# Fused adaLN, attention and gated MLP on one core: how the first modulation weights and V's weights are read and used

## The chip, the core and the metric

The kernel runs on one core of a Trainium2 chip. A core has a matrix engine (TensorE, "PE" in the profile; its weight loads are shown as "PEld"), a vector engine (VectorE, "DVE"), a scalar engine (ScalarE, "ACT"), a general engine (GpSimd, "POOL") and a sync engine (SyncE, "SP") that issues most transfers. Each engine works through its own list of instructions in order; an instruction that waits holds up all that stand behind it on that engine. Matrix products land in PSUM, which has eight banks; everything else lives in SBUF or in device memory. The metric is the device time of one execution in microseconds (us).

## The reference

With one sequence of 2048 rows, width 448 and 16 heads of 28:

```python
mod = silu(c) @ w_mod            # c: 1x448, w_mod: 448 x 6*448, six parts sa, ca, ga, sb, cb, gb
h = layernorm(x) * (1 + ca) + sa
x = x + ga * attention(h)        # attention(h): qkv = h @ wqkv, softmax over 2048 keys, @ wo
h = layernorm(x) * (1 + cb) + sb
x = x + gb * gated_mlp(h)
```

Everything is float32. The change concerns the first pair of parts, sa and ca, and the product of the first 512 rows of h with the columns of wqkv that make V.

## The kernel before

The kernel's order of work is written out by hand: the instructions of each engine run in the order in which the program issues them. The rows of x are taken in four groups of 512 (four tiles of 128 rows). The start, up to the first product for q and k, does this for group 0:

- `load_x(0)` (L178) brings the four tiles of x: tiles 0 and 1 by one transfer each from ACT's queue, tiles 2 and 3 together from SP's. `load_mod(0)` (L173) brings the part of w_mod for (sa, ca) as four blocks `wm` of 112x896, one for each 112 of the 448 entries of c; each block has all 448 columns of sa and of ca. Four transfers of V's weights (`load_w("v", i)`, chunks of 128 rows of wqkv in the order 0, 2, 1, 3, the last one 64 rows in two transfers) follow on SP, and then group 1 of x and the first columns of the weights of q and k (`load_w("a", i)`).
- `ln_stat`, `ln_rs`, `ln_norm` (L274 to L298) make the layer norm: means and variances on DVE, the power -1/2 on POOL, the normalization on DVE, and a copy of 64 columns on ACT. `tp_first` (L369) transposes tile by tile on PE into the four banks `tps[0..3]`, one for each chunk of 128 columns.
- The modulation columns: the product silu(c) @ w_mod is a sum over the four blocks. The first block is scaled on ACT (L380), blocks 1 and 2 are added on DVE for all 896 columns (`mod_acc`, L241), block 3 chunk by chunk (`mod_last`, L407). `mod_dot` (L420) sums over the 112 partitions on PE by a product with ones, and `mod_cols` (L427, L429) brings the result from PSUM into `col_ca` and `col_sa` on DVE. A chunk's columns can therefore be ready only after all four blocks have come.
- h itself is kept as a rounded high part and a low remainder (fp32r), in `hT[0]`, whose slots 0, 1, 2, 6 hold the high parts of chunks 0 to 3 and slots 3, 4, 5 the remainders of chunks 0 to 2 (slot 6 holds both for the short chunk 3). `h_hi` (L441) makes the high part on ACT, `h_full` (L436) the full value on DVE, `h_lo` (the helper `sub`, L84) the remainder. V's weights are split in the same way into `wv`: `wv_hi` (L354 on ACT, L352 on POOL for chunk 2) and `wv_lo` (`sub`, L84, on DVE).
- `v_step` (L477) runs the products for V: eleven pairs of slots, four row tiles each, 44 matrix products of 128x448. The order `order` goes through high parts first: pairs (0,0), (2,2), (1,1) and then the pairs with remainders.
- Between these, `pe_fill` (L230) lets PE multiply x by ones with no use made of the result: 14 such products at the start, and 5, 2, 2 and 4 later. Each is two passes of PE.

Then `qk_unit` (L323) begins the products for q and k, and the attention and the MLP follow.

Of the kernel before, what the change touches and what calls it, by code (L numbers as in the profile page):

```python
# [8 lines left out]
F32 = mybir.dt.float32  # L9
# [24 lines left out]
def tile_adaln_mha_gmlp(ctx, tc, x, wqkv, wo, w_in, w_spT, b_sp, w_out, cT, w_mod, out):  # L34
# [22 lines left out]
    cols = {}  # L57
# [5 lines left out]
    heapF = dpool.tile([128, 4 * 896], F32R, name="heapF", tag="heapF")  # L63
# [16 lines left out]

    wqk = Halves(4, hview(heapD[2], 0, 4, 896), hview(heapF, 0, 4, 896))
# [85 lines left out]
    def bank(name):  # L167
        k = mode[0](name) if mode[0] else banks[0]
        banks.remove(k)
        banks.append(k)  # L170
        return ring.tile([128, 512], F32, name=name, tag=f"b{k}")

    def load_mod(pair, eng):  # L173
        for k in range(4):
            wms[pair, k] = e1.tile([112, 2, D], F32, name="wm", tag=("wm", "wm", "raw")[pair], bufs=4)
            eng.dma_start(wms[pair, k], w_mod[:, pair, k])

    def load_x(g, eng):  # L178
        xg = e1.tile([128, 4, D], F32, name="xg")
        for t0, t1 in ((0, 1), (1, 2), (2, 4)) if g == 0 else ((0, 4),):  # L180
            (act if t1 - t0 == 1 else eng).dma_start(xg[:, t0:t1, :], x[g, :, t0:t1])
        for t in range(4):
            xts[4 * g + t] = xg[:, t, :]
# [4 lines left out]
    def load_w(kind, i, eng):  # L188
        c0, n, tag = PARTS[kind]
        raw = e1.tile([128, 2 * D], F32, name="raw", tag=tag, bufs=4)[:, :n]  # L190
        if i < 3:
            eng.dma_start(raw, wqkv[i * 128 : (i + 1) * 128, c0 : c0 + n])
# [32 lines left out]
    pcs = {c: bank("pc") for c in (0, 2)}  # L225
    wu = bank("wu")

    def pe_fill(n, with_):
        for _ in range(n):
            pe.matmul(wu[:, 0:128], with_[:, 0:128], ones, start=True, stop=True)  # L230
# [118 lines left out]
    def wv_hi(i):  # L349
        h = wv[:, i if i < 3 else 6, :]  # L350
        if i == 2:
            pool.tensor_copy(h, raws["v", i])  # L352
        else:
            act.activation(h, raws["v", i], AF.Copy)  # L354
# [8 lines left out]


    tps, fs = {}, {}
# [3 lines left out]
    def tp_first(t):  # L369
        for c in range(4):  # L370
            pe.transpose(tps[c][:, t * 128 : (t + 1) * 128], xn1[0][t][:, c * 128 : (c + 1) * 128], ident)

    x0, x3 = xts[0], xts[3]
    pe_fill(14, x0)
    ln_stat(0, (0, 1))
    ln_rs(0, 0, 2)
    ln_stat(0, (2, 3))
    ln_rs(0, 2, 4)
    accs[0] = e2.tile([112, 2, D], F32, name="acc")
    act.activation(accs[0], wms.pop((0, 0)), AF.Copy, scale=silu[:, 0:1])  # L380
    ln_norm(0, (0, 1))
    mod_acc(0, 1)
    tp_first(0)
    tp_first(1)
    ln_norm(0, (2, 3))
    mod_acc(0, 2)
    pe_fill(5, x3)
    tp_first(2)
    tp_first(3)
    pe_fill(2, x3)  # L390

    acc0 = [stage.tile([128, 512], F32, name="acc0", tag="qh")[0:112] for _ in range(2)]
    wm3 = wms.pop((0, 3))

    def mod_last(c):
        for part in (1, 0):
            if c < 3:
                o = acc0[part][:, c * 128 : (c + 1) * 128]  # L400
                a, w = (v[:, part, c * 128 : (c + 1) * 128] for v in (accs[0], wm3))
            else:
                o = acc0[part][:, 384:512].rearrange("p (r n) -> p r n", n=64)
                a, w = (
                    v[:, part, 384:D].rearrange("p (r n) -> p r n", r=1).broadcast_to([112, 2, 64]) for v in (accs[0], wm3)
                )
            dve.scalar_tensor_tensor(out=o, in0=w, scalar=silu[:, 3:4], in1=a, op0=ALU.mult, op1=ALU.add)  # L407

    def mod_dot(c, which):
        if c == 1:  # L410
            pcs[c] = ps_o.tile([128, 512], F32, name="pc", tag="o")
        if c == 3:
            pcs[c] = pcs[1][:, 2:4]
        for i, part in enumerate((1, 0)):
            cs = slice(c * 128, (c + 1) * 128)
            if which == "C":
                o, lhs, rhs = 2 + i, wm3[:, part, cs], silu[:, 3:4]
            else:
                o, lhs, rhs = i, (accs[0][:, part] if which == "A" else acc0[part])[:, cs], ones[:112, 0:1]
            pe.matmul(pcs[c][:, o : o + 1], lhs, rhs, start=True, stop=True)  # L420

    def mod_cols(c):
        for i, (nm, plus1) in enumerate((("ca", 1.0), ("sa", 0.0))):
            o = cols[nm][:, c : c + 1]
            if c == 0:
                a, b = pcs[c][:, i : i + 1], pcs[c][:, 2 + i : 3 + i]
                dve.tensor_scalar(out=o, in0=a, scalar1=b, scalar2=plus1, op0=ALU.add, op1=ALU.add)  # L427
            else:
                dve.tensor_scalar(out=o, in0=pcs[c][:, i : i + 1], scalar1=plus1, scalar2=None, op0=ALU.add)  # L429

    def h_full(c):
        if c < 2:
            fs[c] = e1.tile([128, 512], F32, name="hfull")
        else:
            fs[c] = stage.tile([128, 512], F32, name="hfull", tag="qf")
        dve.tensor_scalar(  # L436
            out=fs[c], in0=tps[c], scalar1=cols["ca"][:, c : c + 1], scalar2=cols["sa"][:, c : c + 1], op0=ALU.mult, op1=ALU.add
        )
# [11 lines left out]

    for i in (0, 2, 1, 3):
        load_w("a", i, sp)
    wv_hi(0)
    wv_hi(2)
    mod_dot(0, "C")
    mod_dot(0, "A")
    mod_last(2)
    pe_fill(2, x3)
    mod_dot(2, "all")
    pe_fill(4, x3)  # L460
    mod_cols(0)
    h_hi(0)
    mod_cols(2)
    h_hi(2)
    mod_last(1)
    mod_last(3)
    wv_hi(1)
    wv_lo(0, dve)


    order = [STEPS[j] for j in (0, 1, 6, 2, 3, 4, 7, 5, 8, 9, 10)]
    pvs = [(kt, bank("pv") if kt < 3 else None) for kt in range(4)]
# [9 lines left out]
    mod_dot(1, "all")  # L482
    mod_cols(1)
    h_hi(1)
    wv_hi(3)
    v_step(1, (0, 1, 2))
    mod_dot(3, "all")
    wv_lo(2, dve)
    h_full(0)
    mod_cols(3)  # L490
    h_hi(3)
    v_step(2, (0, 1, 2))
    pvs[3] = (3, ps_o.tile([128, 512], F32, name="pv", tag="o"))
    for j in range(3):
        v_step(j, (3,))
    h_lo(0, pool)
    h_full(2)
    h_full(1)
    wv_lo(1, dve)
    h_lo(2, dve)  # L500
    h_lo(1, dve)
    h_full(3)
    h_lo(3, dve)
    wv_lo(3, dve)
# [3 lines left out]
    for j in range(3, NST):  # L508
        v_step(j, range(4))

# [976 lines left out]
```

## Time and profile before

| | |
|---|---|
| median of 3 runs | 1396.61 us (1396.61 to 1398.2) |
| profiled execution, span from first to last instruction | 1394.0 us |
| busy: PE, PEld, DVE, ACT, POOL | 1386.8, 988.9, 1027.5, 776.5, 285.5 us |
| first product of PE that uses data (a transpose) | 8.51 us |
| first product for V | 14.90 us |
| first product for q and k | 25.08 us |
| mean rate of the transfers, 0 to 25.24 us | 280 GB/s |

The profile shows one execution. Rows of a group give the source line, engine, operation, output and inputs with their shapes, the number of instructions, their busy time and the mean length of one in ns, and then the engine's idle time just before them with what ended it. Rows of a timeline begin with start and length in us. A busy PE is not a PE at its peak. The runs' time is 2.6 us above the span of the profiled execution: 1396.61 - 1394.0, what lies before the first and behind the last instruction.

### The profile page before, as it was taken

The numbers are of one execution on the slowest core, as the hardware profiler recorded it, in microseconds if no ns is written. First come the engines' busy times: TensorE is split into PE (matmuls) and PEld (weight loads), VectorE is DVE, ScalarE is ACT, GpSimd is POOL, SyncE is SP. The second block draws the span as 40 slices with busy tenths as digits, with TensorE's granted clock in tenths as the row PEclk, the third lists the DMA queues.
The fourth block names the chain that finished last, engine by engine and source line by source line (L and its number), as shares of the span: only waits on it lengthen the run. The fifth ranks groups of instructions, "written<-read, shape, count | busy, mean of one in ns | idle before, by whom it ended". The sixth has DMA issues, their size and how long they took to land.

```text
span 1394.0 us, 20327 instructions
## 1 busy us (share of the span) xinstructions
PE 1386.8 (99%) x7180; PEld 988.9 (71%) x7180; DVE 1027.5 (74%) x1741; ACT 776.5 (56%) x1490; POOL 285.5 (20%) x306
## 2 busy tenths in 40 slices
PE   8999999999999999999999999999999999999999
PEld 8888655555555555555555555988998888888888
DVE  7798888888888888888888851750366655668574
ACT  4623677777766667777777779363234544434211
POOL 2234213221224143323200021000142330000000
PEclk9999999999999999999999999999999999999999
DMA  8564644565465556554323002434103333445453
GB/s 265 150 178 177 196 109 151 172 177 154 149 178 167 162 159 189 165 161 150 111 68 76 21 18 73 161 123 140 46 4 110 113 109 112 143 137 163 142 174 110
DMA packets 99377, 187.01 MB, mean 134 GB/s; under 512 B 17736, under 2 KB 29130, under 8 KB 96730
## 3 DMA queue, kind: packets, MB, share of 16 engines
q1 hardware_dynamic: 96558, 181.42, 42.6%
q10 hardware_dynamic: 2718, 4.30, 0.9%
q8 instruction: 56, 0.92, 0.3%
q14 instruction: 45, 0.37, 0.1%
HBM read 130.42 MB, written 50.46 MB: 130 GB/s over the span
## 4 chain that ended last, share of the span: by engine, by line
PE 99%; DMA 0%; DVE 0%; ACT 0%; ACTq 0%; issue 0%
PE st_ps L666 19%; PE o_ps L681 17%; PE mt L634 17%; PE acc L1250 7%; PE acc L1252 7%; PE acc L1251 7%; PE z_ps L1176 5%; PE pq L323 5%; PE z_ps L1062 5%; PE wo_ps L928 3%; PE pv L305 2%; PE y_ps L1357 2%; PE y_ps L1358 2%; PE y_ps L1356 2%; PE tp L117 1%; PE pv L477 1%
## 5 line engine op out<-in xcount | busy, mean ns | idle before, releaser
L639 DVE TENSOR_REDUCE pm<-mt 128x1 f32<-128x512 f32 x1024 | 631.1, 682 | 85.6 <-PE mt L634 85.5
L670 ACT ACTIVATE P<-st_ps 128x512 f32<-128x512 f32 x1024 | 514.5, 628 | 200.8 <-PE st_ps L666 200.7
L666 PE MATMUL st_ps<-qst,kst 128*128 128x512 f32 x1024 | 404.1, 406 | 0.0
L634 PE MATMUL mt<-kst,qst 128*128 128x512 f32 x1024 | 401.7, 392 | 0.0
L666 PEld LDWEIGHTS st_ps<-qst,kst 128*128 128x128 f32 x1024 | 191.2, 187 | 141.2 <-issue 93.1
L681 PE MATMUL o_ps<-P,V 128*32 128x512 f32 x2048 | 247.1, 598 | 0.0
L634 PEld LDWEIGHTS mt<-kst,qst 128*128 128x128 f32 x1024 | 192.4, 188 | 31.8
L791 POOL TENSOR_TENSOR ws_raw<-ws_raw 128x512 f32<-128x512 f32 x80 | 103.2, 1290 | 293.8 <-DMA ws_raw<-in_w_spT_dram 290.9
L1138 ACT ACTIVATE wsp_h<-raw_sp 128x512 fp32r<-128x512 f32 x112 | 70.0, 630 | 153.6 <-PE acc L1252 102.9
L84 DVE TENSOR_TENSOR wsp_l<-raw_sp,wsp_h 128x512 fp32r<-128x512 f32 x112 | 80.7, 730 | 83.1 <-ACT wsp_h L1138 82.3
L681 PEld LDWEIGHTS o_ps<-P,V 128*32 128x32 f32 x2048 | 54.7, 109 | 122.0 <-issue 114.0
L1250 PE MATMUL acc<-wsp_h,heapA 128*128 128x512 f32 x224 | 87.3, 390 | 0.0
L1251 PE MATMUL acc<-wsp_l,heapA 128*128 128x512 f32 x224 | 87.2, 389 | 0.0
L1252 PE MATMUL acc<-wsp_h,heapA 128*128 128x512 f32 x224 | 87.2, 389 | 0.0
L1251 PE MATMUL acc<-wsp_l,heapB 128*128 128x512 f32 x174 | 67.7, 389 | 0.0
L1252 PE MATMUL acc<-wsp_h,heapB 128*128 128x512 f32 x174 | 67.7, 389 | 0.0
L1250 PE MATMUL acc<-wsp_h,heapB 128*128 128x512 f32 x174 | 67.7, 389 | 0.0
L323 PE MATMUL pq<-heapD,heapD 128*128 128x512 f32 x196 | 61.8, 390 | 0.0
L1180 DVE BATCH_NORM_STATS2 stz<-z 128x6 f32<-128x448 f32 x32 | 19.9, 625 | 50.4 <-ACT z L1179 30.1
L1250 PEld LDWEIGHTS acc<-wsp_h,heapA 128*128 128x128 f32 x224 | 42.0, 188 | 8.9 <-DVE cD L1256 0.3
L1252 PEld LDWEIGHTS acc<-wsp_h,heapA 128*128 128x128 f32 x224 | 42.0, 188 | 8.8
L1251 PEld LDWEIGHTS acc<-wsp_l,heapA 128*128 128x128 f32 x224 | 42.0, 188 | 8.6
(222 smaller groups left out, 1597.0 us busy)
## 6 DMA issues: line engine op xcount, KB each, us to landing
ws_raw<-in_w_spT_dram SPq DMA_DIRECT2D x160, 256.0 KB
ws_scr<-ws_raw SPq DMA_DIRECT2D x80, 256.0 KB
raw_sp<-ws_scr SPq DMA_DIRECT2D x80, 256.0 KB
kst<-qk_scr SPq DMA_DIRECT2D x45, 224.0 KB
qst<-qk_scr SPq DMA_DIRECT2D x45, 224.0 KB
raw_sp<-in_w_spT_dram SPq DMA_DIRECT2D x32, 256.0 KB
qk_scr<-qh SPq DMA_DIRECT2D x28, 256.0 KB
qk_scr<-ql SPq DMA_DIRECT2D x28, 256.0 KB
```

The source lines that it names most:

```text
L84: eng.tensor_tensor(out=dst, in0=a, in1=hi.bitcast(F32), op=ALU.subtract)
L323: pe.matmul(pq, wqk[:, b, m * 128 : (m + 1) * 128], hT[g][:, a, :], start=j == 0, stop=j == NST - 1)
L634: pe.matmul(mt, qst[h % 3][:, t * 128 : (t + 1) * 128], kst[h % 3][:, kb * 512 : (kb + 1) * 512], start=True, stop=True)
L639: dve.tensor_reduce(out=pms[h][:, t, kb : kb + 1], in_=mt, axis=AX.X, op=ALU.max)
L666: pe.matmul(st, kst[h % 3][:, kt * 128 : (kt + 1) * 128], qst[h % 3][:, qb * 512 : (qb + 1) * 512], start=True, stop=True)
L670: act.activation(p, st, AF.Exp, scale=SCALE)
L681: pe.matmul(otile[h][32 * qb : 32 * qb + 32, :], V[:, kt, h, :], ptiles.pop((u, qb)), start=kt == 0, stop=kt == NT - 1)
L791: pool.tensor_tensor(out=a, in0=a, in1=b, op=SUMS[i // 16][2])
L1138: act.activation(hi, raw, AF.Copy)
L1250: pe.matmul(acc[i], zh, hi, start=st == 0, stop=False)
L1251: pe.matmul(acc[i], zh, lo, start=False, stop=False)
L1252: pe.matmul(acc[i], zl, hi, start=False, stop=st == 7)
```

## The change

The first part of w_mod (for sa and ca) is stored by column chunks: chunk c has, for each of the 112 partitions, all four blocks k and both parts of its 128 columns (64 for chunk 3), in one piece of 4096 bytes (2048). Its four transfers alternate with those of V's weights on SP: chunk 0, V's rows 0, chunk 2, V's rows 2, chunk 1, V's rows 1, chunk 3, V's rows 3. Tiles 1, 2 and 3 of x come by one SP transfer each, and tile 0 alone by ACT's queue. The chunks lie in a new tile `wm0`, in the place (`heapF`) that half of the weights of q and k takes later; `heapF` and its memset of 64 rows therefore come after V's products.

Chunk 0 of the modulation is made by PE alone (`mod_direct`: eight products, four blocks for each part, with silu as the moving operand). The other chunks are scaled on ACT (`acc_first`) and summed on DVE (`acc_rest`, three instructions of 112x256 one upon the other; for chunk 3 four of 112x128), then summed over the partitions on PE as before. V's weights are split by POOL alone, four casts and four subtractions in a row. `h_full` moves from DVE to ACT, and `h_lo(0)` from POOL to DVE. V's pairs run chunk by chunk, the one for chunk 1 with chunk 1's columns, which stand between. Of `pe_fill` only 13 products at the start are left. The loads of the first weights for q and k and of group 2 of x stand behind the last `h_lo`. All instructions after the first products for q and k stand as before.

```diff
 def load_x(g, eng):
     xg = e1.tile([128, 4, D], F32, name="xg")
-    for t0, t1 in ((0, 1), (1, 2), (2, 4)) if g == 0 else ((0, 4),):
-        (act if t1 - t0 == 1 else eng).dma_start(xg[:, t0:t1, :], x[g, :, t0:t1])
+    for t0, t1 in ((0, 1), (1, 2), (2, 3), (3, 4)) if g == 0 else ((0, 4),):
+        (act if t1 == 1 else eng).dma_start(xg[:, t0:t1, :], x[g, :, t0:t1])
...
+    def load_mod0(c, eng):
+        n = 128 if c < 3 else 64
+        wms[0, c] = wm0[0:112, c * 1024 : c * 1024 + 8 * n].rearrange("r (k p n) -> r k p n", k=4, p=2)
+        eng.dma_start(wms[0, c], w_mod0[c * 1024 * 112 : (c * 1024 + 8 * n) * 112].rearrange("(r k p n) -> r k p n", k=4, p=2, n=n))
...
-    load_mod(0, sp)
     for i in (0, 2, 1, 3):
+        load_mod0(i, sp)
         load_w("v", i, sp)
     load_x(1, sp)
     pool.memset(wv[64:128, 7, :].bitcast(F32), 0.0)
-    pool.memset(wqk[64:128, 7, 0:896].bitcast(F32), 0.0)
...
     def wv_hi(i):
-        h = wv[:, i if i < 3 else 6, :]
-        if i == 2:
-            pool.tensor_copy(h, raws["v", i])
-        else:
-            act.activation(h, raws["v", i], AF.Copy)
+        pool.tensor_copy(wv[:, i if i < 3 else 6, :], raws["v", i])
...
+    def mod_direct(c):
+        wm = wms.pop((0, c))
+        for i, part in enumerate((1, 0)):
+            for k in range(4):
+                pe.matmul(pc_of(c, i), wm[:, k, part, :], silu[:, k : k + 1], start=k == 0, stop=k == 3)
+
+    def acc_first(c):
+        n = 128 if c < 3 else 64
+        o = acc0[c] = stage.tile([128, 512], F32, name="acc0", tag="qh")[0:112, 0 : 2 * n].rearrange("p (a n) -> p a n", n=n)
+        act.activation(o, wms[0, c][:, 0], AF.Copy, scale=silu[:, 0:1])
+
+    def acc_rest(c):
+        wm, o = wms.pop((0, c)), acc0[c]
+        for k in (1, 2, 3):
+            if c == 3 and k == 3:
+                break
+            dve.scalar_tensor_tensor(out=o, in0=wm[:, k], scalar=silu[:, k : k + 1], in1=o, op0=ALU.mult, op1=ALU.add)
...
-        dve.tensor_scalar(
-            out=fs[c], in0=tps[c], scalar1=cols["ca"][:, c : c + 1], scalar2=cols["sa"][:, c : c + 1], op0=ALU.mult, op1=ALU.add
-        )
+        act.activation(fs[c], tps[c], AF.Identity, scale=cols["ca"][:, c : c + 1], bias=cols["sa"][:, c : c + 1])
...
+    x0 = xts[0]
+    pe_fill(13, x0)
+    for t in range(4):
+        ln_stat(0, (t,))
+        if t % 2:
+            ln_rs(0, t - 1, t + 1)
     for i in (0, 2, 1, 3):
-        load_w("a", i, sp)
...
+        wv_hi(i)
+        wv_lo(i, pool)
+    mod_direct(0)
+    ln_norm(0, (0, 1))
+    for t in (0, 1):
+        for c in range(4):
+            tp_first(c, (t,))
+    acc_first(2)
+    ln_norm(0, (2, 3))
+    for c in (0, 2, 1, 3):
+        tp_first(c, (2, 3))
+    mod_cols(0)
+    acc_rest(2)
     h_hi(0)
...
+    acc_first(1)
+    acc_rest(1)
+
+    order = [(0, 0), (0, 3), (3, 0), (2, 2), (2, 5), (5, 2), (1, 1), (1, 4), (4, 1), (6, 6), (6, 7)]
+    pvs = [(kt, bank("pv")) for kt in range(2)]
+    pvs.append((2, ps_o.tile([128, 512], F32, name="pv", tag="o")))
...
     v_step(0, (0, 1, 2))
+    h_full(0)
+    mod_dot(2)
+    mod_cols(2)
+    h_hi(2)
+    h_lo(0, dve)
+    v_step(1, (0, 1, 2))
+    mod_dot(1)
+    mod_cols(1)
+    v_step(2, (0, 1, 2))
+    h_full(2)
+    h_lo(2, dve)
+    acc_first(3)
+    acc_rest(3)
+    mode[0] = lambda name: tp0_bank
+    pvs.append((3, bank("pv")))
+    mode[0] = None
+    for j in range(3):
+        v_step(j, (3,))
+    h_hi(1)
+    h_full(1)
+    h_lo(1, dve)
+    v_step(3, range(4))
+    mod_dot(3)
+    mod_cols(3)
+    h_hi(3)
+    h_full(3)
+    h_lo(3, dve)
+    for i in (0, 2, 1, 3):
+        load_w("a", i, sp)
     load_x(2, sp)
     for i in (0, 2, 1, 3):
         load_w("b", i, sp)
-    for j in range(3, NST):
+    for j in range(4, NST):
         v_step(j, range(4))
+
+    heapF = dpool.tile([128, 4 * 896], F32R, name="heapF", tag="heapF")
+    wqk = Halves(4, hview(heapD[2], 0, 4, 896), hview(heapF, 0, 4, 896))
+    pool.memset(wqk[64:128, 7, 0:896].bitcast(F32), 0.0)
```

More of the change, by code (lines that the diff above doesn't have):

```diff
@@ L377, in tile_adaln_mha_gmlp, with pc_of @@
[L377 to L403, printed above, removed]
+    def pc_of(c, i):
+        return wu[:, 256 + 2 * c + i : 257 + 2 * c + i]
@@ L404, in mod_last @@
                 a, w = (
-                    v[:, part, 384:D].rearrange("p (r n) -> p r n", r=1).broadcast_to([112, 2, 64]) for v in (accs[0], wm3)
+                    v.rearrange("p (r n) -> p r n", r=1).broadcast_to([112, 2, 64]) for v in (o[:, part], wm[:, 3, part])
                 )
[L407 to L413, printed above, removed]
-        for i, part in enumerate((1, 0)):
[L415 to L420, printed above, removed]
+                dve.scalar_tensor_tensor(out=d, in0=w, scalar=silu[:, 3:4], in1=a, op0=ALU.mult, op1=ALU.add)
```

74 lines of the change are left out of this document (22 added, 52 removed).

## The prediction

> **What bounds the kernel now.** I read the chain that ended last, then the busy times by stage, then the timeline of the start, and last the places late in the kernel where DVE and POOL work side by side.
>
> ```profile
> PE 99%; DMA 0%; DVE 0%; ACT 0%; ACTq 0%; issue 0%
> ```
> ```profile
> 0.00:25.24 25.24, 21.49 (x135) 20.31 (x136) 19.40 (x52) 10.20 (x19) 6.94 (x15) 1.00 0.91 280
> 25.24:85.00 59.76, 59.76 (x303) 52.83 (x303) 48.81 (x78) 35.11 (x70) 15.86 (x16) 1.00 0.63 174
> 150.00:860.00 710.00, 710.00 (x3995) 408.56 (x3998) 591.38 (x1002) 509.20 (x1015) 167.25 (x178) 1.00 0.45 133
> ```
> ```profile
> 3.61 5.06 PE L230 MATMUL wu<-ones,xg 128*128 128x128 f32 x28 [3.61 <-DMA xg<-in_x_dram]
> 10.92 1.10 PE L371 MATMUL tp<-ident,xn 128*128 128x128 f32 x8
> 12.30 0.51 PE L420 MATMUL pc<-silu,wm 112*128 112x1 f32 x4
> 13.37 0.56 POOL L352 CAST wv<-raw 128x448 fp32r<-128x448 f32 x1 [3.96 <-DMA raw<-in_wqkv_dram]
> 13.74 1.54 ACT L441 ACTIVATE heapD<-tp,col_sa,col_ca 128x512 fp32r<-128x512 f32 x2 [0.84 <-DVE col_sa L427]
> 14.90 0.85 PE L477 MATMUL pv<-wv,heapD 128*128 128x448 f32 x3
> 17.22 8.02 PE L477 MATMUL pv<-wv,heapD 128*128 128x448 f32 x38
> 25.08 2.91 PE L323 MATMUL pq<-heapD,heapD 128*128 128x512 f32 x12
> ```
>
> PE makes the whole chain, and from 25.24 to 860 us it is never idle (59.76 of 59.76, 710 of 710). Nothing behind the first q/k product (25.08) is reordered, so the time changes by what that product moves, as long as nothing later becomes late. PE's 21.49 busy us before it hide its slack: 28 of the passes, and later ones, are fills. V's products start at 14.90, behind the last block of w_mod, and run without interruption only from 17.22: 38 in 7.86 us (25.08 - 17.22), 0.207 each.
>
> **The change part by part.**
>
> *Transfers.* The landing times of before can be read off what waited for them:
>
> ```profile
> 5.72 0.63 DVE L279 BATCH_NORM_STATS2 st<-xg 128x6 f32<-128x448 f32 x1 [0.92 <-DMA xg<-in_x_dram]
> ...
> 5.40 0.33 SPq L192 DMA_DIRECT2D raw<-in_wqkv_dram  x1
> 7.77 0.47 SPq L88 DMA_DIRECT2D raw<-in_wqkv_dram  x1
> 9.20 0.34 SPq L181 DMA_DIRECT2D xg<-in_x_dram  x1
> 10.70 2.10 SPq L192 DMA_DIRECT2D raw<-in_wqkv_dram  x3
> 12.32 0.58 ACT L354 ACTIVATE wv<-raw 128x448 fp32r<-128x448 f32 x1 [0.74 <-DMA raw<-in_wqkv_dram]
> wm<-in_w_mod_dram SPq DMA_DIRECT2D x12, 392.0 KB
> ```
>
> SP's issue at 5.40 waited for tiles 2 and 3 of x, those at 7.77 and 9.20 for blocks 0 and 1 of w_mod: 392 KB in 1.43 us. At this rate chunk 0 (448 KB) takes 1.64; behind x, all of which is there by 5.7 (DVE waited for tile 1 until 5.72), that is 7.4. Each 224 KB of V's weights takes 0.82. So V 0 lands at 8.2, chunk 2 at 9.8, V 2 at 10.6, chunk 1 near 12.3, V 1 13.1, chunk 3 13.9, V 3 14.7. Check: chunk 1 is complete after 2688 KB, as V 0 was before, and that was used at 12.32. Two more transfers of x cost SP some 0.4 us each of issue, early and under transfers in flight. The loads for q and k, now queued behind group 1 of x, need only old transfers to land; their issue began at 10.70 before and ends by some 15 us now, and the first is used after 20.
>
> *PE to V's first product.* Passes of PE from the stage rows:
>
> ```profile
> 4.00:6.00 2.00, 2.00 (x11) 2.00 (x11) 1.05 (x4) 0.00 (x0) 0.00 (x0) 1.00 1.07 354
> 10.00:12.00 2.00, 2.00 (x19) 1.85 (x18) 2.00 (x4) 0.52 (x2) 0.00 (x0) 1.00 1.03 300
> ```
>
> Passes take about 0.2 us at first and 0.11 later. The 28 passes of fill ended near 8.5 (3.61 + 5.06, less the tail of the last); 26 end at 8.3. `mod_direct` is 16 passes, to 10.1, and chunk 0 is there long before 8.3. Transposes of tiles 0 and 1 are 8 passes, chunk 0's of tiles 2 and 3 two more: 11.2. `h_hi(0)` then runs 11.5 to 12.3 on ACT (0.78 below), V starts at 12.35 instead of 14.90. ACT's `acc_first(2)` waits for chunk 2 (9.8) with the copies for tiles 2 and 3 behind it; they end near 10.8, and PE needs them at 11.7. Hidden with 0.9 to spare.
>
> *DVE, ACT and POOL.* Durations:
>
> ```profile
> L241 DVE SCALAR_TENSOR_TENSOR acc<-wm,silu,acc 112x896 f32<-112x896 f32 x2 | 2.3, 1150 | 0.5 <-DMA wm<-in_w_mod_dram 0.5
> L407 DVE SCALAR_TENSOR_TENSOR acc<-wm,silu,acc 112x128 f32<-112x128 f32 x6 | 1.7, 345 | 0.0
> L436 DVE TENSOR_SCALAR hfull<-tp,col_ca,col_sa 128x512 f32<-128x512 f32 x4 | 3.1, 804 | 0.0
> L441 ACT ACTIVATE heapD<-tp,col_sa,col_ca 128x512 fp32r<-128x512 f32 x4 | 3.1, 778 | 1.7 <-DVE col_sa L429 0.8 <-DVE col_sa L427 0.8
> L354 ACT ACTIVATE wv<-raw 128x448 fp32r<-128x448 f32 x3 | 1.7, 570 | 0.7 <-DMA raw<-in_wqkv_dram 0.7
> L84 DVE TENSOR_TENSOR wv<-raw,wv 128x448 fp32r<-128x448 f32 x3 | 1.9, 617 | 0.0
> L84 POOL TENSOR_TENSOR heapD<-wo_raw,heapD 128x448 fp32r<-128x448 f32 x3 | 3.5, 1154 | 0.2
> L290 DVE TENSOR_SCALAR xn<-xg,mv,rs 128x448 f32<-128x448 f32 x4 | 1.8, 500 | 0.0
> ```
>
> DVE loses four `h_full` (3.2) and four subtractions for V's weights (2.5), and its sums change from 2 of 896 columns and 8 of 128 to 6 of 256 and 4 of 128. A 112x256 sum is not in the trace; between 345 and 1150 ns the line gives 0.48. ACT gets four `h_full` at about 0.78 and drops three casts at 0.57. POOL gets four casts (0.56) and four subtractions at 1.15 instead of 0.62.
>
> First with each engine undisturbed. Chunk 2's sums run from 10.6 to 12.1. `acc_first(1)` on ACT stands behind `h_hi(0)` and ends at 12.55; three dependent sums end at 14.15. Products (0,0) end at 12.95, chunk 2's dots at 13.3, (0,3) at 13.95; chunk 1's dots wait to 14.2. On DVE `mod_cols(2)` stands behind chunk 1's sums; its columns are ready at 14.4, `h_hi(2)` and `h_full(2)` on ACT end at 15.95, `h_lo(2)` at 16.6, chunk 3's four sums at 17.9. PE has done pairs to (2,2) by 17.1, waits for chunk 3's dots until 18.3, and has 28 products left: 5.8. First q/k product 24.1, a **gain of 1.0**. V's low weights are never late here: POOL has the first at 9.9, wanted at 13.3.
>
> But POOL's splits and DVE's sums run at the same time, which they did not before:
>
> ```profile
> 61.01 2.31 POOL L84 TENSOR_TENSOR acc_l<-acc,acc_h 112x448 fp32r<-112x448 f32 x2 [7.94 <-ACT acc_h L250]
> 62.76 1.10 DVE L84 TENSOR_TENSOR heapD<-hfull,heapD 128x512 fp32r<-128x512 f32 x1 [1.57 <-ACT heapD L131]
> 64.10 0.69 DVE L84 TENSOR_TENSOR heapD<-hfull,heapD 64x512 fp32r<-64x512 f32 x1 [0.24 <-ACT heapD L131]
> ...
> 1095.45 1.01 POOL L1144 TENSOR_TENSOR z<-z 128x384 f32<-128x384 f32 x1 [34.32 <-DVE heapA L84]
> 1095.54 1.47 DVE L84 TENSOR_TENSOR wsp_l<-raw_sp,wsp_h 128x512 fp32r<-128x512 f32 x1 [0.23 <-ACT wsp_h L1138]
> ...
> 1055.78 1.28 DVE L84 TENSOR_TENSOR wsp_l<-raw_sp,wsp_h 128x512 fp32r<-128x512 f32 x2
> 1056.99 1.21 DVE L84 TENSOR_TENSOR heapB<-z,heapB 128x384 fp32r<-128x384 f32 x3
> 1058.60 0.68 DVE L84 TENSOR_TENSOR wsp_l<-raw_sp,wsp_h 128x512 fp32r<-128x512 f32 x1
> 1056.00 5.13 POOL L1144 TENSOR_TENSOR z<-z,z 128x384 f32<-128x384 f32 x2 [1.89 <-DVE z L1189]
> ```
>
> A subtraction that takes 0.68 alone took 1.47 at 1095.54: POOL's ended at 1096.46, and DVE's 0.55 us later. The same at 62.76, behind POOL's end at 63.32. The other way, two POOL operations of 1.01 took 5.13 while DVE went from one to the next without a gap to 1059.28. So one engine works while the other stands, and an engine that has its next operation ready does not let the other in.
>
> The nearest unseen case is the sum (scalar_tensor_tensor) beside POOL; below, its price is nothing (the gain above), and above, it behaves like the subtraction. I take the second, since both read two SBUF tiles. The Trainium skill ("SBUF — State Buffer", "Who interferes with whom") says that a vector instruction with two SBUF inputs and a GpSimd instruction that reads SBUF exclude each other for a whole instruction, which would take in the sums. By its words alone the second engine waits for one instruction, which is the milder order of the two below; the row at 1056.00 shows it waiting for several.
>
> Now the work on both together. From 8.5 us there are POOL's three casts and three subtractions that come first and the last cast (3 x 1.71 + 0.56 = 5.7), two normalizations (0.9) and six sums (2.9): 9.5 us in a row, so the last of chunk 1's sums ends at 18.0 instead of 14.15. Every sum needs the one before it, and at each such gap POOL comes in; POOL's cast follows its subtraction without a gap. If DVE gets in after each single POOL operation, the last cast and some of a subtraction fall behind the sums: 17.2. POOL is through by 17.1, and what follows on DVE, ACT and PE keeps its distances: **3.05 to 3.85 us later than the undisturbed course**. That is 2.1 to 2.8 above 25.08.
>
> *Behind V.*
>
> ```profile
> L279 DVE BATCH_NORM_STATS2 st<-xg 128x6 f32<-128x448 f32 x8 | 4.8, 604 | 0.9 <-DMA xg<-in_x_dram 0.9
> 26.71 1.33 POOL L108 TENSOR_TENSOR rs<-rs,mhalf 128x4 f32<-128x4 f32 x1
> ```
>
> DVE ends `h_lo(3)` near 24.9 and needs 2.9 for group 1's four statistics (0.60 and a small step each) and 2.6 for the low weights of q/k. POOL's power (1.33, and its first step) then ends near 31, and four normalizations at 33.1. PE wants the transposes after 22 q/k products of some 0.23 (12 last 2.91 in the row at 25.08, the tail of the last included), near 32.8. Between 0 and 0.5 us more. The memset of `heapF`, 0.8 on POOL, comes after its last split and is wanted 6 us later. I put the whole at **+2.9**.
>
> The sum: 1394.0 + 2.9 = 1396.9 of span, 2.6 outside it as before, 1399.5.
>
> **The rivals.**
>
> *A. No exclusion for the sums.* Then the gain of 1.0 stands: 1395.6. For it: no row shows a sum beside a long POOL operation. Against: the subtraction's rows.
>
> *B. PE alone decides.* If DVE's and ACT's chains are shorter than worked out, V's 44 products (9.1) and 6 dots (1.1) run from 12.35 without a wait to 22.5: -2.6, 1394.0. Against: five waits on three engines would have to vanish.
>
> *C. PE slows down.* The 13 fills behind 8.5 us go, 26 passes, and under the forecast PE stands for up to 2.8 us at a time. If its passes fall back to the 0.2 us of the first stretch for 3.5 us, 1.75 is added: 1401.2. The trace shows the slow stretch only at the start. In the Trainium skill ("TensorE: Matmul & The Clock Gate", "Part 1: The HAM clock gate") the slow clock is the default and comes back after an idle window of about 3.4 us; no run here shows that.
>
> *D. The chunks come no earlier.* If 4096-byte pieces move slower than 3584-byte ones and chunk 0 lands after 9.5, all shifts 1.2 more: 1400.7. Against: 392 KB in 1.43 us is 281 GB/s, and the stage's mean over all sizes is 280.
>
> **How the numbers follow.** Forecast 0.65, own range 1398.6 to 1400.6; A 0.13, B 0.08, C 0.10, D 0.04. A change of less than 0.2% (2.8 us, so 1393.8 to 1399.4) is about what a measurement of this kernel cannot tell from none. Slower by more: 0.6 of the forecast (0.39), C and half of D: 0.51. Faster by more: some of B and what A may be off, 0.06. The rest, 0.43, is the same. The range takes in A below and C above: 1395.4 to 1401.2.
>
> **What would show it.** Right: V's first product near 12.4; sums of 112x256 longer than 0.6 us in the mean; PE idle before the dots of chunks 2 and 1, 2 to 4 us in total, and before chunk 3's, some 0.9; first q/k product at 27 to 28. Sums at 0.48 and a first q/k product near 24 would show A. Passes of 0.2 us after 8 us show C, chunk 0's products after 9.5 D. Wrong altogether is the prediction if PE is idle anywhere behind 33 us where it was not before.

## The result, and the profile after

| | before | after |
|---|---|---|
| median of the runs | 1397.10 us (9 runs) | 1400.69 us (1400.12 to 1401.85, 9 runs) |
| ratio after / before, 95% interval | | 1.0025 [1.0016, 1.0035] |
| profiled execution, span | 1394.0 us | 1398.7 us |
| first V product / first q/k product | 14.90 / 25.08 us | 14.10 / 28.23 us |
| mean TensorE clock | 1.000 in the profile | 0.996 to 0.998 in all 9 runs |

The changed kernel is 3.6 us slower. In the profiles the first q/k product came 3.15 us later. Below, *sums* are the additions on DVE that make a chunk's modulation columns (`acc_rest`), *dots* are PE's products with ones behind them (`mod_dot`), and *splits* are the casts and subtractions of V's weights. The busy times by stage of the changed kernel; the columns are the stretch, its length, the busy time of PE, PEld, DVE, ACT and POOL with their instruction counts, the granted clock, the DMA share and GB/s:

```profile
0.00:28.39 28.39, 22.68 (x115) 20.97 (x116) 19.23 (x49) 11.40 (x22) 13.19 (x22) 0.88 0.89 251
28.39:85.00 56.61, 56.61 (x289) 49.98 (x288) 45.11 (x73) 34.64 (x69) 12.66 (x14) 1.00 0.58 165
```

Behind the first q/k product PE is full again (56.61 of 56.61). Ahead of it two numbers moved: the transfers run at 251 GB/s (before 280), and the granted clock is 0.88 (before 1.00). The same view with the stretches set to the changes of the clock:

```profile
7.88:11.29 3.41, 3.01 (x28) 2.85 (x27) 2.07 (x8) 0.51 (x2) 2.33 (x4) 1.00 1.05 250
11.29:14.70 3.41, 3.41 (x18) 3.31 (x17) 2.28 (x5) 1.58 (x4) 2.53 (x3) 0.50 1.04 234
14.70:18.12 3.42, 2.32 (x14) 1.60 (x12) 3.05 (x7) 2.04 (x4) 1.99 (x4) 1.00 1.05 275
18.12:21.53 3.41, 2.90 (x8) 2.63 (x9) 3.31 (x8) 2.21 (x4) 2.33 (x2) 0.50 1.06 361
21.53:28.20 6.67, 6.67 (x36) 6.19 (x35) 4.68 (x14) 3.38 (x6) 0.84 (x1) 1.00 0.81 263
```

Twice the clock stood at half for 3.41 us. The timeline of the same start (start, length, engine, line, and in brackets the idle time before with what ended it):

```profile
3.71 5.13 PE L231 MATMUL wu<-ones,xg 128*128 128x128 f32 x26 [3.71 <-DVE ec L223]
...
9.23 1.92 PE L376 MATMUL wu<-silu,wm 112*128 112x1 f32 x16 [0.40 <-DMA wm<-in_w_mod_dram]
...
11.01 3.40 PE L367 MATMUL tp<-ident,xn 128*128 128x128 f32 x16
...
11.93 0.51 ACT L381 ACTIVATE acc<-wm,silu 112x256 f32<-112x256 f32 x1 [2.70 <-DMA wm<-in_w_mod_dram]
...
12.47 2.56 DVE L388 SCALAR_TENSOR_TENSOR acc<-wm,silu,acc 112x256 f32<-112x256 f32 x3 [1.06 <-ACT acc L381]
...
14.10 1.13 PE L455 MATMUL pv<-wv,heapD 128*128 128x448 f32 x3
14.79 0.51 ACT L381 ACTIVATE acc<-wm,silu 112x256 f32<-112x256 f32 x1 [0.84 <-DMA wm<-in_w_mod_dram]
...
15.33 1.70 DVE L388 SCALAR_TENSOR_TENSOR acc<-wm,silu,acc 112x256 f32<-112x256 f32 x3 [0.30 <-ACT acc L381]
...
16.83 1.19 POOL L82 TENSOR_TENSOR wv<-raw,wv 128x448 fp32r<-128x448 f32 x1
...
17.09 1.48 DVE L82 TENSOR_TENSOR heapD<-hfull,heapD 128x512 fp32r<-128x512 f32 x1
...
17.22 0.60 PE L400 MATMUL wu<-ones,acc 112*128 112x1 f32 x4 [0.80 <-DVE col_sa L404]
...
18.62 3.62 PE L455 MATMUL pv<-wv,heapD 128*128 128x448 f32 x10 [0.80 <-DVE heapD L82]
...
19.45 1.62 DVE L388 SCALAR_TENSOR_TENSOR acc<-wm,silu,acc 112x128 f32<-112x128 f32 x2
...
21.11 0.61 DVE L396 SCALAR_TENSOR_TENSOR acc<-wm,silu,acc 112x128 f32<-112x128 f32 x2
...
22.09 0.50 PE L400 MATMUL wu<-ones,acc 112*128 112x1 f32 x4
...
22.45 5.95 PE L455 MATMUL pv<-wv,heapD 128*128 128x448 f32 x28
...
28.23 1.09 PE L324 MATMUL pq<-heapD,heapD 128*128 128x512 f32 x4
```

Read from the end: 28 products at full clock run back to 22.45. Chunk 3's dots at 22.09 wait for nothing, because PE itself is late: its ten products from 18.62 took 3.47 us (to 22.09), most of it at half clock. They could start only when `h_lo(0)` was done, which took 1.48 us beside POOL's 16.83 row. `h_lo(0)` stood on DVE behind chunk 1's sums, and these behind chunk 1's landing, which ACT used at 14.79. From 15.33 to 21.7 DVE hardly pauses. Three losses therefore lie in one chain: late chunks, DVE held up beside POOL, and half clock. DVE was done with chunk 3's sums at 21.72 (21.11 + 0.61), only 0.37 before the dots, so a faster PE alone would have met DVE's wait almost at once.

### The profile page after: what moved, and what is told of

The parts are those of the page before. It is cut to its first block, busy times and chain, and to the rows that moved or that the text cites. A ratio compares the mean times of both kernels' runs of the same rounds, so it can differ in the third digit from the quotient of the medians.

```text
span 1398.7 us, 20288 instructions
## 1 busy us (share of the span) xinstructions
PE 1389.3 (99%) x7160; PEld 989.7 (71%) x7160; DVE 1026.9 (73%) x1736; ACT 777.3 (56%) x1493; POOL 289.2 (21%) x312
## 4 chain that ended last, share of the span: by engine, by line
PE 98%; DMA 1%; DVE 0%; SPq 0%; issue 0%; ACT 0%
PE st_ps L654 19%; PE o_ps L669 17%; PE mt L622 17%; PE acc L1239 7%; PE acc L1240 6%; PE acc L1238 6%; PE z_ps L1164 5%; PE pq L324 5%; PE z_ps L1050 5%; PE wo_ps L916 3%; PE pv L306 2%; PE y_ps L1345 2%; PE y_ps L1346 2%; PE y_ps L1344 2%; PE tp L115 1%; DMA wm<-in_w_mod_dram 1%
```

## The experiments

The times below are compared with runs of the kernel before that were taken beside them. "q/k" is the start of the first q/k product in the one profiled execution; its own time can lie at either end of the runs, so q/k and median need not agree within 1 us.

| kernel | median, us | before, us | difference | ratio [95%] | q/k, us |
|---|---|---|---|---|---|
| after | 1400.69 | 1397.10 | +3.59 | 1.0025 [1.0016, 1.0035] | 28.23 |
| e1 fillers in the dots' bank | 1401.57 | 1397.39 | +4.18 | 1.0030 [1.0019, 1.0042] | 30.59 |
| e2 splits moved | 1399.09 | 1397.39 | +1.70 | 1.0014 [1.0005, 1.0023] | 27.74 |
| e3 = e1 + e2 | 1400.48 | 1397.39 | +3.09 | 1.0022 [1.0012, 1.0032] | 28.13 |
| e4 x loaded as before | 1400.36 | 1397.39 | +2.97 | 1.0022 [1.0013, 1.0030] | 28.43 |
| e5 before, no later fillers | 1399.12 | 1397.18 | +1.94 | 1.0012 [1.0003, 1.0022] | 27.79 |
| e6 fillers, own banks | 1400.10 | 1397.18 | +2.92 | 1.0020 [1.0011, 1.0028] | 27.23 |
| e7 = e2 + e4 | 1397.50 | 1397.18 | +0.32 | 1.0000 [0.9991, 1.0009] | 26.61 |
| e8 = e7, steps reordered | 1398.43 | 1397.18 | +1.25 | 1.0005 [0.9996, 1.0014] | 25.55 |
| e9 = e8, two waits removed | 1395.97 | 1396.77 | -0.80 | 0.9995 [0.9986, 1.0004] | 25.29 |
| e10 = e7 + fillers, own bank | 1396.18 | 1396.77 | -0.59 | 0.9996 [0.9987, 1.0005] | 26.06 |
| e12 after, again | 1400.45 | 1397.95 | +2.50 | 1.0019 [1.0009, 1.0028] | 29.76 |

**e1, fillers.**

```diff
-    pe_fill(13, x0)
+    pe_fill(16, x0)
     mod_direct(0)
+    pe_fill(3, x3)
...
     v_step(1, (0, 1, 2))
+    pe_fill(6, x3)
     mod_dot(1)
+    pe_fill(5, x3)
```

> The changed kernel with filler products put back where TensorE waits: 16 instead of 13 at the start, 3 behind chunk 0's products, 6 and 5 around the dots of chunk 1. Theory 1 (VectorE's queue sets the course: sums and h_lo(0) held up by GpSimd's splits, so that chunk 3's last sum ends at 21.7 whatever TensorE does): the granted clock stays 1.0 from 8 us on and V's ten products behind h_lo(0) take 2.1 us instead of 3.4, but chunk 3's dots still come at 21.8 and the first q/k product at 27.8 to 28.0 (28.23 without fills), time 0.2 to 0.4 us below the changed kernel. Theory 2 (the half clock sets the course): the first q/k product at 26.5 to 26.9 and the time 1.3 to 1.7 us below the changed kernel. Theory 3 (late transfers set it): 28.0 to 28.3, no change.

The timeline of e1:

```profile
17.32 2.71 PE L231 MATMUL wu<-ones,xg 128*128 128x128 f32 x12 [1.45 <-DVE col_sa L404]
...
19.82 0.85 PE L400 MATMUL wu<-ones,acc 112*128 112x1 f32 x4
...
20.54 1.58 PE L231 MATMUL wu<-ones,xg 128*128 128x128 f32 x10
...
22.15 0.16 DVE L404 TENSOR_SCALAR col_ca<-wu 128x1 f32<-128x1 f32 x1 [3.48 <-PE wu L231]
```

None of the three expectations was met (q/k 30.59, time above the changed kernel's). The fillers write the same tile `wu` as the dots. They waited for DVE's read of chunk 2's columns (1.45 us), and DVE's read of chunk 1's columns waited 3.48 us for the last filler (22.15), though the dots had started at 19.82. The fillers meant to cover idle time became a wait. The clock still fell once, from 17.59 to 21.01. This run says nothing on what the clock costs; e3, with the same fillers, has the same flaw.

**e2, V's splits out of the way.**

```diff
     def wv_hi(i):
-        pool.tensor_copy(wv[:, i if i < 3 else 6, :], raws["v", i])
+        act.activation(wv[:, i if i < 3 else 6, :], raws["v", i], AF.Copy)
...
+    wv_hi(0)
+    wv_lo(0, pool)
     acc_first(2)
...
     mod_dot(3)
+    heapF = dpool.tile([128, 4 * 896], F32R, name="heapF", tag="heapF")
+    wqk = Halves(4, hview(heapD[2], 0, 4, 896), hview(heapF, 0, 4, 896))
+    pool.memset(wqk[64:128, 7, 0:896].bitcast(F32), 0.0)
+    for i in (2, 1, 3):
+        wv_lo(i, pool)
...
-    order = [(0, 0), (0, 3), (3, 0), (2, 2), (2, 5), (5, 2), (1, 1), (1, 4), (4, 1), (6, 6), (6, 7)]
+    order = [(0, 0), (0, 3), (3, 0), (2, 2), (5, 2), (1, 1), (4, 1), (2, 5), (1, 4), (6, 6), (6, 7)]
```

The casts of chunks 2 and 1 stand on ACT behind `h_full(0)`, that of chunk 3 behind `h_full(1)`. The memset of `heapF` waits for chunk 3's sums and so holds back the three subtractions.

> The changed kernel with V's weights cast on ScalarE and only their first low part subtracted on GpSimd before the sums; the other three low parts follow on GpSimd behind chunk 3's sums, and V's steps take the low parts later. GpSimd and VectorE then share no time between 12.4 and 21 us. Theory 1 (the shared port): sums of 112x256 at 0.48 us each instead of a mean of 0.69, h_lo(0) at 0.68 instead of 1.48, chunk 3's sums done at 19.5 to 20.0 instead of 21.72; but the ten products at half clock then end near 21.0, so the first q/k product comes at 27.0 to 27.4 and the time is 0.8 to 1.2 us below the changed kernel. Theory 2 (the half clock): the first q/k product at 27.9 to 28.3, time the same to -0.3. Theory 3 (late transfers): the same as theory 2.

The groups of DVE's start by shape (count, busy time, mean ns), first of the changed kernel:

```profile
L388 DVE SCALAR_TENSOR_TENSOR acc<-wm,silu,acc 112x256 f32<-112x256 f32 x6 | 4.1, 686 | 1.5 <-ACT acc L381 1.4
...
L82 DVE TENSOR_TENSOR heapD<-hfull,heapD 128x512 fp32r<-128x512 f32 x3 | 3.0, 986 | 0.0
...
L388 DVE SCALAR_TENSOR_TENSOR acc<-wm,silu,acc 112x128 f32<-112x128 f32 x2 | 1.6, 790 | 0.0
```

and of e2:

```profile
L388 DVE SCALAR_TENSOR_TENSOR acc<-wm,silu,acc 112x256 f32<-112x256 f32 x6 | 2.9, 484 | 3.0 <-ACT acc L381 2.8
...
L82 DVE TENSOR_TENSOR heapD<-hfull,heapD 128x512 fp32r<-128x512 f32 x3 | 2.1, 685 | 0.7 <-ACT hfull L411 0.7
...
L388 DVE SCALAR_TENSOR_TENSOR acc<-wm,silu,acc 112x128 f32<-112x128 f32 x2 | 0.7, 349 | 0.0
```

With POOL out of the way these eleven operations lose 1.2 + 0.9 + 0.9 = 3.0 us and stand at their undisturbed lengths: sums do share in the exclusion. (The edit also moves casts and steps, so its time is not the exclusion's alone; the lengths of the single operations are.) But the profile's q/k came only 0.5 earlier, since DVE then waited for ACT and chunk 1 (2.8 us): in this execution chunk 1 was used only at 15.64, and chunk 3's sums ended at 21.42 in place of the 19.5 to 20.0 that theory 1 expected. The clock stayed 1.000 in the profile but not in all executions. Seven of the 11 had a mean clock of 0.999 or more, with a median time of 1398.67; four had 0.998 or less, median 1401.13.

**e3, both.**

> Both edits at once (the fillers, and V's splits out of the way of the sums). If the shared port and the half clock each hide the other, the two together give more than their sum: chunk 3's dots at 19.8 to 20.2, the first q/k product at 25.8 to 26.2, the time 2.0 to 2.5 us below the changed kernel and 0.9 to 1.5 above the one before. If only one of them counts, the result is that of the better single edit to within 0.3 us.

Neither case came: q/k at 28.13, time 3.09 above the kernel before, no gain over e2, for the reason found in e1 (`h_lo(2)` came at 19.83 in place of 19.42). Nothing on the additivity of the two follows.

**e4, x as before.**

```diff
-        for t0, t1 in ((0, 1), (1, 2), (2, 3), (3, 4)) if g == 0 else ((0, 4),):
-            (act if t1 == 1 else eng).dma_start(xg[:, t0:t1, :], x[g, :, t0:t1])
+        for t0, t1 in ((0, 1), (1, 2), (2, 4)) if g == 0 else ((0, 4),):
+            (act if t1 - t0 == 1 else eng).dma_start(xg[:, t0:t1, :], x[g, :, t0:t1])
```

> The changed kernel with x's first group loaded as in the kernel before (tiles 0 and 1 by ScalarE's queue, the pair by SyncE's). Theory 3 in its first form (the order of x's loads made the chunks late): chunk 0 lands by 8.2 to 8.6 instead of 9.12, chunk 1 by 13.9 to 14.2 instead of 14.75, the first q/k product 0.5 to 0.9 earlier, time 0.5 to 0.9 below the changed kernel. Second form (the rate of the chunks' packets, 272 ns for 4096 bytes, makes them late): landings of chunk 1 on within 0.3 us of the changed kernel, time the same to -0.3. Theories 1 and 2 expect nothing beyond what the landings give.

Two rows of e4, one of the groups and one of the timeline:

```profile
L388 DVE SCALAR_TENSOR_TENSOR acc<-wm,silu,acc 112x256 f32<-112x256 f32 x6 | 5.9, 988 | 0.1
```
```profile
10.48 0.51 ACT L381 ACTIVATE acc<-wm,silu 112x256 f32<-112x256 f32 x1 [1.03 <-DMA wm<-in_w_mod_dram]
```

Chunk 2 is used 1.45 us earlier (10.48), chunk 1 1.8 earlier (12.97). One pair of executions would not settle it, but all profiles of this study do: with x loaded as before the transfers of the first 5 us ran at 202 to 215 GB/s (eight profiles), in the order of the change at 151 to 164 (six). Chunk 1 was used at 12.85 to 14.29 us in the five of the eight that have the new chunks, and at 14.09 to 15.64 in the six, 1.3 us later in the mean. So the order of x's loads did make the chunks late. The time hardly moved, and q/k did not come earlier as expected: DVE now had sums to do all the while POOL split V's weights, and a sum took 0.988 us in place of 0.686. Chunk 1's sums ended at 17.80, in the changed kernel at 17.03. In this profile the exclusion took what the transfers gave.

**e5, the kernel before without its later fillers** (`pe_fill(5, x3)`, both `pe_fill(2, x3)` and `pe_fill(4, x3)` left out).

> The kernel before, without the 13 filler products behind its first 14 (5, 2, 2 and 4 of them); nothing else of the change. If the fillers are what keeps the clock (rival C of the prediction), the granted clock falls to half in one or two windows of 3.4 us between 9 and 22 us in most executions (mean clock 0.997 to 0.999 instead of 1.000), and the time is 1.3 to 3 us above the kernel before. If they only fill time that is idle anyway, the clock stays 1.000 and the time is the same to within 0.5 us.

Windows of e5:

```profile
7.74:14.56 6.82, 4.73 (x38) 4.07 (x37) 5.99 (x16) 3.19 (x7) 2.05 (x4) 1.00 1.07 273
14.56:21.39 6.83, 6.58 (x21) 6.07 (x22) 5.22 (x14) 4.38 (x8) 1.29 (x1) 0.50 1.02 325
```

This is the clean test of the clock: same order, same transfers, 13 fillers less. V's first product came at 14.81 (before 14.90), then 6.83 us at half clock, q/k at 27.79, and the mean clock was 0.996 to 0.999 in all 11 executions. The time rose by 1.94 us, interval 0.4 to 3.1 (ratio times 1397). The fillers are not idle work; in this order they keep the clock. (0.999 alone does not say so: it also appears in runs of the kernel before. 10 of the 11 lay at 0.998 or below.)

**e6, fillers in banks of their own.** As e1 without the three added at the start; the three behind chunk 0 write to `tps[3]` ahead of the transposes, and five before and five behind chunk 1's dots to the bank of V's fourth tile.

> The changed kernel with fillers again, but written to banks that nothing else uses at that time (3 behind chunk 0's products, 5 before and 5 behind the dots of chunk 1), so that no reader of the dots stands behind them. Theory 2 (the half clock costs): mean clock 0.999 or 1.000 in nearly all executions, V's ten products behind h_lo(0) in 2.1 us, time 1.0 to 2.0 us below the changed kernel. Theory 1 (VectorE's queue alone): chunk 3's dots still at 21.7 to 21.9, time 0.1 to 0.5 us below the changed kernel. If the fillers still hold something up, the first q/k product comes later than 28.3 and the time rises.

```profile
18.86 2.27 PE L456 MATMUL pv<-wv,heapD 128*128 128x448 f32 x10
...
20.98 0.61 PE L400 MATMUL wu<-ones,acc 112*128 112x1 f32 x4
```

The clock was 0.999 or 1.000 in all executions and V's ten products took 2.12 us (20.98 - 18.86) in place of 3.47, as theory 2 had it. Against the kernel before, the time fell by 0.7 (from +3.59 to +2.92), less than theory 2 and more than theory 1 expected, and inside the intervals. Chunk 3's dots came before theory 1's 21.7: this time `h_lo(0)` took 0.93 in place of 1.48 and chunk 3's first two sums 0.7 in place of 1.62. Chunk 3's last sum ended at 20.93, with V's products: while the sums are held up (mean 0.795 here), PE would only wait for DVE in place of running slowly, and a larger gain from the clock alone is not shown.

**e7, e2 and e4 together.**

> V's splits out of the way of the sums (as in e2_split) and x loaded as before (as in e4_x_as_before), no fillers. e4 showed chunk 2 landed at 10.5 instead of 11.9 and chunk 1 at 13.0 instead of 14.8, but its sums of 112x256 then took 1.0 us each under GpSimd's splits. If these two are what hid the gain: sums 0.48 to 0.5 each, chunk 1's sums done by 15.5, h_lo(0) done by 16.6, the first q/k product at 25.8 to 26.6 in an execution at full clock; executions with mean clock 0.999 or above at 1396.8 to 1397.8, those at 0.998 or below 1.2 to 2.7 us longer. If late landings didn't matter: as e2_split, median 1399.1.

Median +0.32 over the kernel before, with an interval of about 1.3 us to either side: the two edits together undo the loss. q/k came at 26.61, at the end of the expected range, and the executions lay between 1396.22 and 1399.43. Each edit alone left +1.70 and +2.97, so they gained 1.9 and 0.6, and together 3.3. (Taken from the second measurement of the changed kernel, +2.50 in e12, it is 0.8, -0.5 and 2.2.) The surplus of the pair over the sum of the two, 0.8 or 1.9, lies inside the noise of four medians; that the two losses hide each other is read from the profiles, where chunk 1's sums ended at 17.03 in the changed kernel, 17.71 in e2, 17.80 in e4 and 15.96 here. What the clock has in the 3.3 is not separated: eight of the 11 executions had a mean clock of 1.000, so the half windows of the changed kernel were mostly gone too. In the profile, one of the other three, one half window was left:

```profile
13.88:17.29 3.41, 2.24 (x15) 1.74 (x14) 2.41 (x8) 3.21 (x6) 0.00 (x0) 1.00 1.06 308
17.29:20.70 3.41, 3.41 (x12) 3.07 (x11) 2.52 (x6) 2.44 (x5) 0.84 (x1) 0.50 1.06 335
```

**e8, reordered** (from e7):

```diff
     mod_dot(2)
     mod_cols(2)
     h_hi(2)
+    h_full(0)
+    acc_rest(1)
...
-    order = [(0, 0), (0, 3), (3, 0), (2, 2), (5, 2), (1, 1), (4, 1), (2, 5), (1, 4), (6, 6), (6, 7)]
+    order = [(0, 0), (0, 3), (2, 2), (3, 0), (1, 1), (5, 2), (4, 1), (2, 5), (6, 6), (1, 4), (6, 7)]
...
+    v_step(4, range(4))
     mod_dot(3)
```

with the cast of chunk 2 ahead of `acc_first(1)`, and the last subtraction on DVE.

> As e7_split_and_x, and the order of the steps follows what is ready: VectorE makes chunk 2's columns before it sums chunk 1, V's steps take chunk 2's high part before chunk 0's low part, and the dots of chunk 3 stand one step later. If what is left over is VectorE's order (PE waiting 1 to 2 us for h_lo(0) and for chunk 3's sums): first q/k product at 24.4 to 25.4 (before: 25.08), executions at full clock at 1396.2 to 1397.4, and fewer half windows since TensorE idles less. If TensorE still waits for the landings: 25.6 to 26.4 and 1397.5 to 1398.3.

q/k was at 25.55, between the two cases, and the median just above the second (1398.43) and above e7's: the reordering alone brought nothing that can be told apart. The earlier q/k does not contradict the longer median: the profiled execution took 1397.2, second fastest of its 11, that of e7 1398.4, second slowest. **e9** takes out two waits that e8's profile shows (DVE 1.20 us ahead of chunk 3's sums, PE 0.59 behind `h_lo(3)`):

```diff
     wv_hi(1)
+    acc_first(3)
     v_step(2, (0, 1, 2))
...
-    order = [(0, 0), (0, 3), (2, 2), (3, 0), (1, 1), (5, 2), (4, 1), (2, 5), (6, 6), (1, 4), (6, 7)]
+    order = [(0, 0), (0, 3), (2, 2), (3, 0), (1, 1), (5, 2), (4, 1), (2, 5), (1, 4), (6, 6), (6, 7)]
```

> e8_reordered with its two visible waits taken out: chunk 3's first term is made on ScalarE before chunk 1's high part (VectorE idled 1.2 us before chunk 3's sums), and V's step with chunk 1's low weights comes before the one with chunk 3's high part (TensorE idled 0.6 us there, at 22.4). If TensorE alone decides from there: dots of chunk 3 at 18.4 to 18.8 instead of 19.06, the first q/k product at 23.8 to 24.6 (before: 25.08; e8: 25.55), time 0.5 to 1.3 us below the kernel before. If the gain of an early first q/k product is given back later (V's rest, the second group's normalization), the time is that of the kernel before to within 0.4 us although the first q/k product is early.

```profile
10.77 1.75 DVE L291 TENSOR_SCALAR xn<-xg,mv,rs 128x448 f32<-128x448 f32 x2 [0.61 <-POOL rs L106]
11.00 1.28 POOL L82 TENSOR_TENSOR wv<-raw,wv 128x448 fp32r<-128x448 f32 x1 [0.26 <-ACT wv L351]
...
12.58 0.98 PE L367 MATMUL tp<-ident,xn 128*128 128x128 f32 x7 [0.91 <-DVE xn L291]
...
20.29 5.16 PE L454 MATMUL pv<-wv,heapD 128*128 128x448 f32 x24
```

PE ran from 20.29 through V's end, but chunk 3's dots (19.92) and q/k (25.29) missed their ranges: chunk 1 was used at 14.29 (e8: 12.85) with the same loads, and the second pair of normalizations took 1.75 us beside POOL's subtraction (0.94 in the changed kernel), so that the transposes waited 0.91. The median, 0.80 below the kernel before, is the lowest of the study and lies in the expected range, though the steps that were to bring it missed theirs; the interval includes no change.

**e10, e7 with five fillers** in the bank of V's fourth tile, ahead of chunk 1's dots.

> e7_split_and_x with five fillers, in a bank of their own, in the 1.1 us in which TensorE waits before the dots of chunk 1; nothing else. If the half clock of e7's profile (17.3 to 20.7 us) is the last loss there: mean clock 1.000 in nearly all executions, V's ten products in 2.1 us instead of 3.5, chunk 3's dots at 19.7 (VectorE's queue) instead of 20.2, the first q/k product at 26.0 to 26.3 instead of 26.6, the median 0.2 to 0.6 below e7's 1397.5. If the clock doesn't matter at this place: the same as e7 to within 0.2.

Mean clock 1.000 in all 11 executions, q/k at 26.06, as forecast. Against the kernel before -0.59, where e7 had +0.32: 0.9 us, more than forecast, with intervals that overlap. The clock can't be the whole of it. A half window of 3.41 us takes 0.0012 off the mean clock of 1397 us, so in e7 only the three executions at 0.999 (median 1398.4) can have had one, and the eight at 1.000 still had a median of 1397.2. So what the five fillers are worth is not shown. e9 and e10 are each some 4 us faster than the changed kernel (3 by its second measurement).

**e11 and e12, both kernels again.**

> The kernel before, profiled a second time, to see what one profile differs from another by itself. TensorE was never idle from 8.7 us on, so its first q/k product should come at 25.0 to 25.2 again and the granted clock stay 1.000. If the 1.4 us that the changed kernel lost between 100 and 822 us (shift 3.2 at 85 us, 4.6 at 822 us) are scatter between executions, this profile is also 0.5 to 2 us behind the first at 822 us; if the change causes them, it agrees with the first to within 0.2 us there.

> The changed kernel, profiled a second time. If the half clock belongs to the kernel and not to one execution: again one to three windows of 3.4 us at half clock between 8 and 22 us, at other places, mean clock 0.996 to 0.998 in all executions. Chunk 1 landed at 14.1 to 15.6 us in the five profiles of this order of loads so far and at 12.9 to 14.3 in the five with x loaded as before: again 14.0 to 15.7. The sums of 112x256 that run beside GpSimd's instructions 0.6 to 1.3 us, the others 0.48. The first q/k product at 27.2 to 28.8, time 3 to 4 us above the kernel before.

e11: q/k at 25.11, clock 1.000, and 0.12 us behind the first profile at 822 us. e12: two half windows again, back to back (16.88 to 23.70), chunk 1 used at 15.48, sums at 0.812 in the mean. The time, +2.50, is less than expected, and two of the ten executions had a mean clock of 0.999. Its q/k, 29.76, lies above the expected range: chunk 0 was late too (products at 9.93), and the half clock covered all ten products behind `h_lo(0)` (19.64 to 23.51). Between 85 and 822 us it fell behind by another 1.0 us (4.69 to 5.68), as the first profile of after did by 1.4, with PE at full clock and busy throughout. This loss is not bound to the new loads and the new order: e5, which has nothing of the change but the missing fillers, lost 0.86 in the same stretch (2.74 to 3.60), e2 0.4, and e9, which has most of the change, nothing (0.85 at both ends). The kernel before is no clean measure of scatter here, since its second profile (1395.88) was faster than all 13 runs taken beside it (1396.32 to 1398.68). The cause of this loss is open.

## Why the prediction was right, and where its steps were not

The time (1399.5 forecast, 1400.69 measured), its sign and the range of 1395.4 to 1401.2 held; the forecast's own range, up to 1400.6, ended just below. The sum came out partly by other terms than those in it, and in part by luck: chunk 1's sums ended at 17.03, close to the forecast's 17.2 to 18.0, but they were late because their chunk was (the first began at 15.33 in place of 12.55), and only 0.25 us of it was the exclusion that the forecast put there.

- *Nothing behind the first q/k product is reordered, so the time moves by its shift.* Right to about 1 us: the shift was 3.15 and the runs' difference 3.59. The span's 4.7 holds besides the open 1.4 us that the profile lost between 85 and 822 us (e12).
- *2.6 us outside the span.* This term was mis-sized: it set the median of three executions against the span of one. In the later runs an execution's own time is 1.7 to 2.0 above its span (1400.51 - 1398.7 = 1.8 for the changed kernel), so the profiled execution of the kernel before took an estimated 1395.8, 1.3 below the median of nine. In medians the forecast was +2.9 and the result +3.59.
- *Transfers.* This step failed. "At this rate chunk 0 takes 1.64; behind x ... 7.4" and chunk 1 "near 12.3" became 9.2 and 14.75. Serial single tiles of x on SP cost more than "some 0.4 us each of issue": the first 5 us ran at 156 GB/s in place of 214, and with x loaded as before chunk 1 was used 1.3 us earlier in the mean (e4). From 5 to 13 us the transfers ran at 256 in place of 289. Whether the longer pieces are slower, as rival D has it, is not shown: the new layout ran at 237 to 275 in its eleven profiles, the old one at 266 to 310 in three. Chunk 0's products began before D's 9.5 in the first profile of the changed kernel and behind it, at 9.93, in the second.
- *V's first product at 12.35.* It came at 14.10. PE's products with chunk 0 began at 9.23 in place of 8.3, and the ten transposes ahead of `h_hi(0)` took 2.2 us (11.01 to 13.18, where `h_hi(0)` began) in place of 1.1, at half clock.
- *The exclusion.* Right in kind: sums at 0.686 in place of 0.484, and e2 shows the difference go with POOL's work. Its place was wrong. The forecast had 9.5 us of joint work in a row from 8.5; with the chunks late there was no such row, and chunk 1's sums cost only 0.2 extra (1.70 against three times 0.484). The price fell on chunk 2's sums (1.1), `h_lo(0)` (0.8) and chunk 3's first sum (0.9). That is 3.0 in all, about the 3.05 to 3.85 forecast, but the 1.1 lay ahead of the wait for chunk 1, so about 1.9 of it stood on DVE's way to chunk 3's dots.
- *PE idle before the dots of chunks 2 and 1, 2 to 4 us, and 0.9 before chunk 3's.* Measured 0.24 and 0.80, another 0.80 ahead of the ten products, and none before chunk 3's, because PE was late itself.
- *Rival C, given 0.10.* Its mechanism was there in all nine executions of the changed kernel (0.996 to 0.998), and in at least eight of the ten of e12, beside the forecast's and not in its place. That was the error in how the cases were set up. Its size is shown only in the old order (1.94, e5); in the new one it lies partly under DVE's wait, and the 0.7 of e6 is inside the intervals.

Had the transfers landed when the forecast said, the exclusion would have cost more (e4's sums, 0.988) and the q/k product would perhaps have come no earlier: e4's 28.43 against 28.23, one execution each. That may be why a wrong landing time did little harm to the sum.

## What to carry to other kernels

Fillers belong to the schedule: leaving 13 out of the old order cost 1.94 us (e5). Take the clock from every execution before and after removing them, and give a new filler a bank that no reader of other results waits on (e1). Work moved to GpSimd was free here only while VectorE did nothing that it excludes; its price has to be read from rows where both are busy. When several losses lie in one chain, undoing one can show little of its worth (0.6 for the loads of x, 1.9 for the splits, 3.3 for both, as far as these medians can tell), so test them in pairs before calling one of them harmless.

## What the runs showed of the hardware beyond this

The clock fell after windows in which TensorE was far from idle: in the changed kernel PE was busy 3.01 of 3.41 us (7.88 to 11.29) before the first half window, in e7 2.24. One window each of e2 and of e12:

```profile
13.56:16.97 3.41, 2.36 (x12) 1.66 (x12) 1.99 (x5) 2.04 (x5) 0.00 (x0) 1.00 1.08 260
```
```profile
13.46:16.87 3.41, 2.38 (x12) 1.46 (x11) 2.80 (x5) 1.69 (x3) 2.10 (x3) 1.00 1.08 234
```

e2's was followed by full clock, e12's by half: the modelled busy time doesn't tell them apart. Counted from the trace, six V products and the dots (2694 columns of moving operands in e7, 2692 in e12) were followed by half clock, and the same with one more transpose (2820 in e2) was not. Three windows make no rule, and a trace can lack single records. The Trainium skill ("TensorE: Matmul & The Clock Gate", "Part 1: The HAM clock gate") gives the slow state after an idle window of about 3.4 us. The length of a window agrees with the 3.41 us here; that it takes an idle one does not.

A normalization with one large SBUF input also took 1.33 us beside POOL's subtraction, against 0.51 alone (e9, the second of the 1.75 row). The Trainium skill ("SBUF — State Buffer", "Who interferes with whom") counts tensor_scalar among the operations that can contend, and the trace agrees.

With identical loads, chunk 1 was used at 12.85 us in e8, where ACT's cast ahead of it set the time, and at 14.29 in e9: an execution's landing times differ by 1.4 us and more, as much as most edits here. From 5 to 13 us the transfers of e8 ran at 275 GB/s, those of e9 at 237; why is open.
